# Keys loaded by tokens, key features ahead of their copies, a reordered head and a transposed last group in a polysketch-attention and ELU-MLP kernel

One core of one Trainium2 chip. The metric is the device time of one execution in microseconds (us), median of several runs. A run's span (first to last recorded activity) is about 1.9 us shorter than its time.

## The reference

```python
def phi(x):                                    # r = 8, head_dim = 32
    a = einsum('rd,bhsd->bhsr', S1, x); b = einsum('rd,bhsd->bhsr', S2, x)
    return einsum('bhsi,bhsj->bhsij', a, b).reshape(..., 64)
q_p, k_p = phi(q), phi(k)                      # q, k, v: (4, 4, 1088, 32), fp32
kv = einsum('bhsf,bhsd->bhfd', k_p, v);  z = sum(k_p, axis=2)
x  = (q_p @ kv) / (q_p . z + 1e-6)             # then heads side by side: (4352, 128)
h  = x @ w_in                                  # w_in (128, 2048), as float64
g  = where(h > 0, h, exp(min(h, 0)) - 1)
out = g @ w_out                                # w_out (2048, 128), as float64
```

The kernel calls the four batches "banks" (b = 0 to 3). S1, S2 and the weights arrive as float64 and are turned into float32 on the chip by integer operations, "rounding" below.

## The kernel before

It works through 9 groups of 512 tokens (the last has 256). One step is one group with one 256-wide piece of the weights: two matmuls into `h`, the ELU on ScalarE and VectorE, and, two steps later, two matmuls into `o`. (The traces show each of these fp32 matmuls as two records.) Names in the traces: `kT` and `qT` are the transposed keys and queries, `abp` the key features in PSUM and `ab` their copy, `kp` their products, `kv` the product with v, `gg` the output of the ELU, `oT` the running sum of `o`. All other work (keys, queries, rounding) is put between steps. Cut to what matters (`# ...` marks cuts):

```python
# keys of bank 0: one queue for each half of the partitions
for i, eng in enumerate((nc.sync, nc.scalar)):
    eng.dma_start(hd["k", 0][64 * i:64 * i + 64]..., k[0, 2 * i:2 * i + 2]...)
load_hd(nc.sync, "q", q, 0, 0, 8)
# ...
load_v(nc.sync, 0)

# the rounding of one piece: A, B (ScalarE), C, D, E; E on GpSimd if pool
order = [(0, 1, 0), (1, 1, 1), (0, 0, 1)] + [(cp, 1, 1) for cp in range(2, NP)]  # piece, w_in, w_out
def RC(i, pool=False):
    round_w(round_c, i); round_w(round_d, i); round_w(round_e, i, pool)

def KF(b, gi):                       # key features of token tiles KG[gi]
    if gi < 2:
        abps[b] = psum.tile([P, 512], F32, name="abp", tag="aux")
    abp = abps[b] if gi < 2 else abps[b][:, 256:]      # gi 2 shares the bank of gi 1
    # ... matmuls into abp, then
    nc.scalar.copy(ab..., abp...)

# last group: o (features on partitions) -> copy -> two transposes -> copy -> two DMAs
nc.vector.tensor_copy(oT[g][:, :n], o)
# ... fin2: transposes into otp, copy to osb
for u in range(2):
    for b, t, i, m in runs(g, u, 0, n):
        nc.sync.dma_start(rows[b, :, t:t + m, :], o[64 * u:64 * u + 64, i:i + m, :])

# what lies between the steps
for n, i in ((2, 3), (3, 4), (5, 5), (6, 6), (8, 7), (9, 8)):
    if i > 3: at(n - 1, RA, i); late(n - 1, RB, i)
    at(n, RC, i, i > 4)
for b in range(1, B):
    at(n - 1, transp, kT, "k", b, 0, NT)
    for i in range(3):
        at(n, KF, b, i); at(n + (i > 0), KO, b, i); at(n + 2, KA, b, i)
    # ...
```

Only one PSUM bank serves `o`; an o that opens a segment waits until the sum before it has been taken out (`oT += o` on VectorE, or a copy).

## Time and profile before

| | before |
|---|---|
| time, median of the 3 runs at hand | 299.99 us (299.66 to 300.33) |
| profiled run | 298.3 us, span 296.4 us |
| TensorE (PE) busy, share of the span | 284.5 us, 96% |
| VectorE (DVE) / ScalarE (ACT) busy | 168.0 / 188.1 us |
| mean granted TensorE clock of the profiled run | 0.991 |

In the timeline views below, a row is start, length, engine, line, operation, tiles, count, and in brackets the idle time before it and what ended it; in the chain views it is start, length, engine, tile, line.

### The profile page before, as it was taken

What the parts mean: (1) busy time and instruction counts of PE and PEld (TensorE: products, weight loads), DVE (VectorE), ACT (ScalarE), POOL (GpSimd) and SP (SyncE); (2) the same over time, 40 slices, a digit from 0 to 9 for tenths busy, and PEclk for the clock granted to TensorE, in tenths of its full rate; (3) what the DMA queues carried; (4) which work ended last, traced back from release to release, by engine and by line L of the source; (5) the groups of instructions that cost most, each with busy time, mean ns of one, the idle gap of its engine ahead of it and who ended that gap; (6) DMA issues with size and microseconds to landing.
All of it is one profiled execution on the core that took longest, in us unless ns stands there. A gap on an engine that the chain in (4) does not pass through costs nothing.

```text
span 296.4 us, 4034 instructions
## 1 busy us (share of the span) xinstructions
PE 284.5 (96%) x1448; PEld 146.0 (49%) x1448; DVE 168.0 (57%) x296; ACT 188.1 (63%) x355; POOL 19.0 (6%) x46
## 2 busy tenths in 40 slices
PE   6879989999999999999999999999999999999993
PEld 4854444544544653445544644444444444444682
DVE  4789999964657275425457274435543554355441
ACT  2249888566467467666646557766666686667681
POOL 1110034620000010000000100000000000000000
PEclk9799999999999999999999999999999999999998
DMA  6942999220110100011001100011002000110010
GB/s 157 339 157 88 198 208 217 39 75 0 18 20 9 30 0 0 3 16 19 1 2 16 21 0 0 1 18 19 0 0 31 8 0 1 17 21 0 6 30 18
DMA packets 37907, 13.37 MB, mean 45 GB/s; under 512 B 32768, under 2 KB 35968, under 8 KB 37888
## 3 DMA queue, kind: packets, MB, share of 16 engines
q1 hardware_dynamic: 37792, 12.84, 19.9%
q10 hardware_dynamic: 96, 0.28, 0.4%
q8 instruction: 11, 0.18, 0.3%
q14 instruction: 8, 0.07, 0.1%
HBM read 10.88 MB, written 2.23 MB: 44 GB/s over the span
## 4 chain that ended last, share of the span: by engine, by line
PE 86%; DVE 8%; DMA 3%; issue 1%; ACT 1%; ACTq 0%; DVEq 0%; SPq 0%
PE o L527 38%; PE h L497 35%; PE kv L300 3%; PE abp L273 2%; PE abwp L367 2%; PE xps L475 2%; PE qtp L460 2%; DMA hd_k<-in_k_dram 2%; DVE gg L514 1%; DMA raw<-in_moe_w_out_dram 1%; DVE W L114 1%; DVE kT L233 1%; DVE raw L119 1%; DVE raw L115 1%; DVE W L101 1%
## 5 line engine op out<-in xcount | busy, mean ns | idle before, releaser
L514 DVE SCALAR_TENSOR_TENSOR gg<-e,h 128x512 f32<-128x512 f32 (+1 forms) x144 | 93.0, 654 | 101.5 <-ACT e L508 101.4
L527 PE MATMUL o<-gg,W 128*128 128x512 f32 (+1 forms) x288 | 130.3, 576 | 0.0
L497 PE MATMUL h<-xg,W 128*128 128x512 f32 (+1 forms) x288 | 128.7, 569 | 0.9 <-ACT xg L446 0.5
L506 ACT ACTIVATE e<-h 128x512 f32<-128x512 f32 (+1 forms) x144 | 81.5, 566 | 23.7 <-PE h L497 23.2
L508 ACT ACTIVATE e<-e 128x512 f32<-128x512 f32 (+1 forms) x144 | 87.3, 606 | 4.5
L497 PEld LDWEIGHTS h<-xg,W 128*128 128x128 f32 x288 | 54.4, 190 | 63.6 <-issue 54.9
L527 PEld LDWEIGHTS o<-gg,W 128*128 128x128 f32 x288 | 52.5, 190 | 52.3 <-issue 48.8
L461 ACT COPY qpT<-qtp 128x512 f32<-128x512 f32 (+1 forms) x16 | 8.3, 562 | 17.1 <-PE qtp L460 17.1
L372 ACT COPY abw<-abwp 128x384 f32<-128x384 f32 (+1 forms) x8 | 3.7, 459 | 23.7 <-PE abwp L367 23.7
L257 DVE TENSOR_TENSOR kp<-ab 128x1024 f32<-128x1024 f32 (+1 forms) x12 | 11.0, 948 | 5.4 <-ACT ab L277 5.4
L277 ACT COPY ab<-abp 128x256 f32<-128x256 f32 (+1 forms) x12 | 3.8, 317 | 12.9 <-PE abp L273 12.6
L273 PE MATMUL abp<-Sab,kT 128*64 128x64 f32 x136 | 7.1, 247 | 3.4 <-DVE Sab L242 1.4
L300 PEld LDWEIGHTS kv<-v,kp 128*64 128x64 f32 (+1 forms) x288 | 9.0, 137 | 2.6 <-issue 2.3
L300 PE MATMUL kv<-v,kp 128*64 128x33 f32 (+3 forms) x288 | 9.7, 224 | 0.0
L390 DVE TENSOR_TENSOR qp<-an,abw 128x1024 f32<-128x1024 f32 (+1 forms) x9 | 9.3, 1046 | 0.3
L273 PEld LDWEIGHTS abp<-Sab,kT 128*64 128x64 f32 x136 | 5.9, 157 | 6.7 <-issue 2.6
L460 PEld LDWEIGHTS qtp<-ident,qp 128*128 128x128 f32 x60 | 7.0, 143 | 4.4 <-issue 2.8
L486 ACT COPY xg<-xps 128x256 f32<-128x256 f32 (+1 forms) x8 | 2.9, 359 | 9.5 <-PE xps L475 9.5
L460 PE MATMUL qtp<-ident,qp 128*128 128x128 f32 x60 | 8.1, 275 | 0.8 <-DVE qp L390 0.8
L320 POOL TENSOR_TENSOR zm<-kvz,zmask 128x32 f32<-128x32 f32 x4 | 1.5, 384 | 112.8 <-issue 64.5
L106 ACT ACTIVATE W<-W,ebias 128x512 uint32<-128x512 uint32 (+1 forms) x9 | 6.0, 672 | 2.7 <-DVE W L101 2.7
L124 POOL TENSOR_TENSOR raw<-raw,tiny 128x512 f32<-128x512 f32 x4 | 5.3, 1318 | 32.0 <-DVE raw L119 31.9
(82 smaller groups left out, 125.0 us busy)
## 6 DMA issues: line engine op xcount, KB each, us to landing
raw<-in_moe_w_in_dram SPq DMA_DIRECT2D x8, 256.0 KB, 6.0
raw<-in_moe_w_out_dram SPq DMA_DIRECT2D x8, 256.0 KB, 6.1
out_dram<-ob SPq DMA_DIRECT2D x104, 16.0 KB, 1.5
hd_k<-in_k_dram SPq DMA_DIRECT2D x3, 544.0 KB, 6.1
hd_q<-in_q_dram SPq DMA_DIRECT2D x3, 544.0 KB, 3.9
v<-in_v_dram SPq DMA_DIRECT2D x12, 72.0 KB, 5.6
v<-in_v_dram SPq DMA_DIRECT2D x12, 64.0 KB, 3.8
v<-in_v_dram SPq DMA_DIRECT2D x1, 288.0 KB, 5.9
```

The costliest lines, as they stand in the source:

```text
L106: nc.scalar.activation(d, d, RELU, scale=8.0, bias=ebias[:dst.shape[0]])
L257: nc.vector.tensor_mul(dst, _ap(a_, list(a_.ap[1:]) + [[0, R]]), _ap(b_, [b_.ap[1], [0, R], b_.ap[2]]))
L273: nc.tensor.matmul(abp[64 * u:64 * u + 64, j * 64:j * 64 + 64], kT[b][:, u * KT + i, :], Sab[:].rearrange("p h y -> p (h y)"), skip_group_ ...
L300: nc.tensor.matmul(kv[64 * hp:64 * hp + 64, g2, :n], kp[:rows, j, h].rearrange("p i j -> p (i j)"), _ap(vt[b][:rows, off:off + D], [[VN - ...
L390: nc.vector.tensor_mul(qp[g][:, h], _ap(a_, list(a_.ap[1:]) + [[0, R]]), _ap(b_, [b_.ap[1], [0, R], b_.ap[2]]))
L460: nc.tensor.transpose(p[:, o:o + P], qp[g][:, r:r + 2].rearrange("p t i j -> p (t i j)"), ident[:])
L461: nc.scalar.copy(qpT[g][:, 2 * hh:2 * hh + 2, :nh, :], p[:, :2 * nh * P].rearrange("p (h m s) -> p h m s", h=2, m=nh))
L497: nc.tensor.matmul(hs[g, cp][c][:, :n], W[:, cp, c * P:c * P + P], xg[g][:, :n])
L506: nc.scalar.activation(e, hs[g, cp][c][:, :n], RELU, scale=-1.0)
L508: nc.scalar.activation(e, e, EXP, scale=-1.0)
L514: nc.vector.scalar_tensor_tensor(gs[g, cp][:, c, :n], es[g, cp][:, c, :n], -1.0, hs[g, cp][c][:, :n], op0=ADD, op1=MAX)
L527: nc.tensor.matmul(ops[g][:, :n], W[:, cp, (2 + c) * P:(3 + c) * P], gg[:, c, :n], start=(first and c == 0), stop=(last and c == 1))
```

## The change

Its intent: get the keys onto the chip in a shape in which VectorE can start on half the tokens, shorten the chain to the first h matmul, remove the wait between key features and their copies, round the w_in half of pieces 2 and 3 before the w_out half, and write the last group with tokens on partitions, so that its transposes go.

```diff
-    for i, eng in enumerate((nc.sync, nc.scalar)):
-        eng.dma_start(hd["k", 0][64 * i:64 * i + 64]..., k[0, 2 * i:2 * i + 2]...)
+    load_hd(nc.sync, "k", k, 0, 0, KT)
+    load_hd(nc.scalar, "k", k, 0, KT, NT)
+    load_hd(nc.sync, "q", q, 0, 0, 8)
+    load_v(0, (nc.sync, nc.scalar))
...
-    order = [(0, 1, 0), (1, 1, 1), (0, 0, 1)] + [(cp, 1, 1) for cp in range(2, NP)]
+    order = [(0, 1, 0), (1, 1, 1), (0, 0, 1), (2, 1, 0), (3, 1, 0), (2, 0, 1), (3, 0, 1)]
+    order += [(cp, 1, 1) for cp in range(4, NP)]
...
+    make_SX()                         # ahead of the key features, no longer behind them
-    def KF(b, gi):
+    def KF(b, part):
+        abp = psum.tile([P, 512], F32, name="abp", tag="aux")
+        # part 0: tiles 0-3; part 1: tiles 4-7 and 8: all matmuls first,
+        # then the copies
...
-        RC(0)                         # the product of piece 0 moves behind the normalisation
+        round_w(round_c, 0); round_w(round_d, 0)
...
+        round_w(round_e, 0)
+        q1(1)
-            nc.scalar.copy(xg[0]...); if tt == 0: q1(1)
+            (nc.scalar.copy if tt else nc.vector.tensor_copy)(xg[0]...)
...
+    def mm2_last(cp, first, last):    # gg stationary, W moving: out has tokens on partitions
+        for a in range(4):
+            c, i = (a % 2, a // 2) if last else divmod(a, 2)
+            nc.tensor.matmul(ops[g][i][:], gg[:, c, i * P:i * P + P], W[:, cp, (2 + c) * P:(3 + c) * P], ...)
+    def fin_last():                   # two half copies, two DMAs on two queues
-    keep_warm(2)
+    keep_warm(1)
-    mm1(0, 0, (0,)) ... mm1(0, 0, (1,))
+    mm1(0, 0)
-    for n, i in ((2, 3), (3, 4), (5, 5), (6, 6), (8, 7), (9, 8)):
+    for n, i in ((2, 3), (3, 4), (4, 5), (4, 6), (5, 7), (6, 8), (8, 9), (9, 10)):
-        at(n, RC, i, i > 4)
+        at(n, RC, i, i > 6)
```

More of the change, by code (lines that the diff above doesn't have):

```diff
@@ L77, in load_hd, with load_v @@
                       src[b].rearrange("h (a c t) d -> (h a) c t d", a=32, c=2)[:, :, t0:t1, :])
-    def load_v(eng, b):
-        for u in range(2):
+    def load_v(b, engs=(nc.sync, nc.sync)):
+        for u, eng in enumerate(engs):
             t0, t1 = u * KT, min(NT, u * KT + KT)
@@ L139 @@
             eng.dma_start(S16[rs, :], src)
-    hd["k", 0] = work.tile([P, 2, NT, D], F32, name="hd_k", tag="hd_k")
-    for i, eng in enumerate((nc.sync, nc.scalar)):
-        eng.dma_start(hd["k", 0][64 * i:64 * i + 64].rearrange("p c t d -> p (c t d)"),
-                      k[0, 2 * i:2 * i + 2].rearrange("h (a x) d -> (h a) (x d)", a=32))
+    load_hd(nc.sync, "k", k, 0, 0, KT)
+    load_hd(nc.scalar, "k", k, 0, KT, NT)
+    load_hd(nc.sync, "q", q, 0, 0, 8)
+    load_v(0, (nc.sync, nc.scalar))
     warm = const.tile([R, 1], F32, name="warm")
@@ L147 @@
     nc.scalar.activation(warm[:], warm[:], EXP)
-    load_hd(nc.sync, "q", q, 0, 0, 8)
     W = const.tile([P, NP, 4 * P], F32, name="W")
@@ L184, in RC @@
         round_w(round_e, i, pool)
-    load_v(nc.sync, 0)
     load_w(0, 0)
@@ L196 @@
         load_hd(nc.sync, "k", k, b, 0, NT)
-        load_v(nc.sync, b)
+        load_v(b)
         load_hd(nc.sync, "q", q, b, 0, NT)
@@ L235, with make_SX @@
     transp(kT, "k", 0, 0, KT)
+    SX = const.tile([P, FD], F32, name="SX")
+    def make_SX():
+        xps = psum.tile([P, 512], F32, name="SXps", tag="aux")
+        nc.tensor.matmul(xps[:, :FD], idr[:].rearrange("p x j -> p (x j)"), Sx[:R].rearrange("p h d -> p (h d)"))
+        nc.scalar.copy(SX[:], xps[:, :FD])
     Sab = const.tile([FD, H, 2 * R], F32, name="Sab")
@@ L244 @@
         nc.gpsimd.tensor_copy(SW[:, b, :, :2, :].rearrange("p h x r -> p h (x r)"), Sab[:])
-    SX = const.tile([P, FD], F32, name="SX")
-    def make_SX():
-        xps = psum.tile([P, 512], F32, name="SXps", tag="aux")
-        nc.tensor.matmul(xps[:, :FD], idr[:].rearrange("p x j -> p (x j)"), Sx[:R].rearrange("p h d -> p (h d)"))
-        nc.scalar.copy(SX[:], xps[:, :FD])
     def outer(dst, ab):
@@ L260 @@
     kvS = const.tile([P, B, H, D], F32, name="kvS")
-    abps, kv_ps, feats, zms, kvz = {}, {}, {}, {}, {}
-    def KF(b, gi):
-        if gi < 2:
-            abps[b] = psum.tile([P, 512], F32, name="abp", tag="aux")
-        abp = abps[b] if gi < 2 else abps[b][:, 256:]
-        tiles = KG[gi]
-        n = len(tiles)
-        rows = P if tiles[-1] + KT < NT else 64
-        for j, i in enumerate(tiles):
-            for u in range(rows // 64):
-                nc.tensor.matmul(abp[64 * u:64 * u + 64, j * 64:j * 64 + 64], kT[b][:, u * KT + i, :],
-                                 Sab[:].rearrange("p h y -> p (h y)"),
-                                 skip_group_check=True, tile_position=(0, 64 * u))
-        ab = work.tile([P, 4, H, 2, R], F32, name="ab", tag="ab", bufs=3)
-        nc.scalar.copy(ab[:rows, :n].rearrange("p t h x r -> p (t h x r)"), abp[:rows, :n * 64])
-        feats[b, gi] = ab, rows
+    kv_ps, feats, zms, kvz = {}, {}, {}, {}
+    def KF(b, part):
+        abp = psum.tile([P, 512], F32, name="abp", tag="aux")
+        todo = []
+        for gi, o in ((1, 0), (2, 256)) if part else ((0, 0),):
+            tiles = KG[gi]
+            rows = P if tiles[-1] + KT < NT else 64
+            for j, i in enumerate(tiles):
+                for u in range(rows // 64):
+                    nc.tensor.matmul(abp[64 * u:64 * u + 64, o + j * 64:o + j * 64 + 64], kT[b][:, u * KT + i, :],
+                                     Sab[:].rearrange("p h y -> p (h y)"),
+                                     skip_group_check=True, tile_position=(0, 64 * u))
+            todo.append((gi, o, rows, len(tiles)))
+        for gi, o, rows, n in todo:
+            ab = work.tile([P, 4, H, 2, R], F32, name="ab", tag="ab", bufs=3)
+            nc.scalar.copy(ab[:rows, :n].rearrange("p t h x r -> p (t h x r)"), abp[:rows, o:o + n * 64])
+            feats[b, gi] = ab, rows
     def KO(b, gi):
@@ L423, in q5_first @@
         KS(0)
-        RC(0)
+        round_w(round_c, 0)
+        round_w(round_d, 0)
         KZ2(0)
@@ L445, in q5_first @@
                 nc.tensor.transpose(q[:, t * P:t * P + P], xn[:, tt, 4 * t:4 * t + 4].rearrange("p m d -> p (m d)"), ident[:])
-            nc.scalar.copy(xg[0][:, 256 * tt:256 * tt + 256], q[:, :256])
-            if tt == 0:
-                q1(1)
+            (nc.scalar.copy if tt else nc.vector.tensor_copy)(xg[0][:, 256 * tt:256 * tt + 256], q[:, :256])
     def q4(g):
@@ L540, in fin1 @@
             nc.scalar.copy(oT[g][:, :n], o)
-        if last and g == NQ - 1:
-            oT[g] = work.tile([P, 512], F32, name="oT", tag="oT")
-            nc.vector.tensor_copy(oT[g][:, :n], o)
-        elif last:
+        if last:
             ob = work.tile([P, 4, 2, 2, D], F32, name="ob", tag="ob", bufs=2)
@@ L553, in fin1 @@
                             nc.sync.dma_start(rows[b, w, q_, :, t:t + m, :], ob[32 * q_:32 * q_ + 32, i:i + m, u, w, :])
-    def fin2(g):
-        n = qn[g]
-        p = psum.tile([P, 512], F32, name="otp", tag="aux")
-        for i in range(n):
-            nc.tensor.transpose(p[:, i * P:i * P + P], oT[g][:, i * P:i * P + P], ident[:])
-        o = work.tile([P, 4, P], F32, name="osb", tag="osb", bufs=1)
-        nc.scalar.copy(o[:, :n].rearrange("p t f -> p (t f)"), p[:, :n * P])
-        rows = out.rearrange("(b y t) f -> b y t f", b=B, t=NT)
-        for u in range(2):
-            for b, t, i, m in runs(g, u, 0, n):
-                nc.sync.dma_start(rows[b, :, t:t + m, :], o[64 * u:64 * u + 64, i:i + m, :])
-    keep_warm(2)
+    def mm2_last(cp, first, last):
+        g = NQ - 1
+        if first:
+            ops[g] = [psum.tile([P, P], F32, name="ol", tag=t, bufs=k) for t, k in (("o", 1), ("aux", 2))]
+        gg = gs.pop((g, cp))
+        for a in range(4):
+            c, i = (a % 2, a // 2) if last else divmod(a, 2)
+            nc.tensor.matmul(ops[g][i][:], gg[:, c, i * P:i * P + P], W[:, cp, (2 + c) * P:(3 + c) * P],
+                             start=(first and c == 0), stop=(last and c == 1))
+    def fin_last():
+        g, n = NQ - 1, qn[NQ - 1]
+        o = work.tile([P, 2, P], F32, name="ol", tag="ol", bufs=1)
+        rows = out.rearrange("(b y t) f -> b y t f", b=B, t=NT)
+        for i, copy in enumerate((nc.scalar.copy, nc.vector.tensor_copy)):
+            copy(o[:, i, :], ops[g][i][:])
+        for u, eng in enumerate((nc.sync, nc.scalar)):
+            b, t = half_tile(g, 0, u)
+            eng.dma_start(rows[b, :, t:t + n, :], o[64 * u:64 * u + 64])
+    keep_warm(1)
     transp(kT, "k", 0, KT, NT)
@@ L574 @@
     q1_first()
-    KF(0, 2)
-    make_SX()
     KO(0, 1)
@@ L585 @@
     q5_first()
-    mm1(0, 0, (0,))
+    mm1(0, 0)
     RA(1)
     RB(1)
-    elu_a(0, 0, 0, (0,))
+    elu_a(0, 0, 0)
     q2(1, 2)
     q4(1)
-    mm1(0, 0, (1,))
-    elu_a(0, 0, 0, (1,))
     RC(1)
@@ L636 @@
         for i in range(3):
-            at(n, KF, b, i)
+            if i < 2:
+                at(n, KF, b, i)
             at(n + (i > 0), KO, b, i)
@@ L650 @@
         at(n + 6, q5, g)
-    done = {}
     N = len(steps)
-    for n in range(N + 4):
+    for n in range(N + 2):
         if 2 <= n < N:
@@ L663 @@
             g2, cp2, first, last = steps[n - 2]
-            if last:
+            if last and g2 < NQ - 1:
                 mm2(g2, cp2, first, last)
                 fin1(g2, cp2 == NP - 1)
-                if cp2 == NP - 1 and g2 == NQ - 1:
-                    done[n + 2] = g2
         if 2 <= n < N:
@@ L672 @@
             f(*a)
-        if 2 <= n < N + 2 and not last:
-            mm2(g2, cp2, first, last)
-        if n in done:
-            fin2(done[n])
+        if 2 <= n < N + 2:
+            if g2 == NQ - 1:
+                mm2_last(cp2, first, last)
+            elif not last:
+                mm2(g2, cp2, first, last)
+    fin_last()
 _INS = ['q', 'k', 'v', 'S1', 'S2', 'moe_w_in', 'moe_w_out']
```

## The prediction

> **What bounds the kernel now.** I read the page first (busy shares, clock slices, chain by engine), then the chain in order of time, then a table of engine busy time by stage, then the timeline of the first 62 us and the last 34.
>
> The page:
>
> ```profile
> PE 284.5 (96%) x1448; PEld 146.0 (49%) x1448; DVE 168.0 (57%) x296; ACT 188.1 (63%) x355; POOL 19.0 (6%) x46
> PEclk9799999999999999999999999999999999999998
> PE 86%; DVE 8%; DMA 3%; issue 1%; ACT 1%; ACTq 0%; DVEq 0%; SPq 0%
> ```
>
> TensorE is the bound: 86% of the chain that ended last. A full step is 1.72 us of h and 1.72 us of o matmuls, and no part of the change removes any of those. So a gain can come only from before the matmul stream starts, from holes in it, and from after its end. The chain in order of time shows these places (start, length, what):
>
> ```profile
> 1.36 4.86 DMA hd_k<-in_k_dram
> 7.81 1.83 PE abp L273 x29
> 11.67 2.42 PE kv L300 x72
> 20.80 1.29 DVE qp L390 x2
> 41.07 1.23 DVE kT L233
> 42.44 1.17 PE abp L273 x32
> 44.38 1.91 PE o L527 x4
> ```
>
> The keys hold everything until 6.2 us. A chain that is mostly VectorE's leads to the stream of h matmuls, which runs without a break from 24.70. At 41 us the chain goes back to VectorE: TensorE has finished the blocks before and waits for the transposed keys of bank 1. Then 32 of the 34 records of key features take 1.17 us, but the next o starts 1.94 us after the first of them. The waits name the reason, and it comes once for each of banks 1 to 3:
>
> ```profile
> PE abp L273 <- ACT ab L277: 1.4, 3, 0.5
> ```
>
> By stage (stretch, its length, busy time of PE, PEld, DVE, ACT, POOL, then clock, DMA share, GB/s):
>
> ```profile
> 7.80:11.60 3.80, 3.33 (x50) 3.05 (x51) 2.81 (x3) 1.22 (x4) 0.27 (x3) 0.55 1.08 327
> 28.00:42.00 14.00, 14.00 (x33) 5.98 (x32) 13.71 (x24) 12.12 (x22) 1.11 (x1) 1.00 0.98 208
> ```
>
> The second row decides my answer: while the weights are rounded, VectorE is busy for 13.71 of 14.00 us beside a full TensorE. There are two bounds there, and VectorE sets when kT of bank 1 is ready. The end of the chain:
>
> ```profile
> 288.61 2.60 PE o L527 x12
> 291.24 0.44 DVE oT L543
> 291.72 0.45 PE otp L559 x2
> 292.19 0.37 ACT osb L561
> ```
>
> After the last o come a copy, two transposes, a second copy and two output DMAs, both issued by SyncE from 292.59 in 1.20 us, each landing 2.0 us after its start.
>
> **What the Trainium skill says.** (1) "PSUM — Partial Sum Buffer", section on bank collisions: two engines must not access one bank and quadrant at once, and a scheduler orders them, reads against writes too. The trace agrees: the last group of key features shares its bank with the group before and waits 0.5 us for ScalarE's copy, three times. (2) "TensorE: Matmul & The Clock Gate", Part 1: the clock is halved after an idle window of about 3.4 us, and the window runs freely. The trace agrees: clock 0.50 from about 7.95 to 11.3 us after a hole at 5.7 to 7.2. (3) The same page, section "LDWEIGHTS (loading the stationary operand)": a load takes time with its columns, about 107 ns for 128. The sixteen loads of the 66-column matmuls quoted below start over 1.86 us, a pitch of 0.117 us each, so it agrees roughly. (4) "DMA: Bandwidth & Descriptors", section "Issuing engines are not separate DMA queues": a second queue saves issue time only, as all share 16 engines. The trace has DMA share 1.0 or more between 4 and 14 us, so I expect nothing of v on two queues but the 0.6 us of one issue on SyncE.
>
> **The change part by part.** *Keys by tokens, v on two queues.* SyncE's half of k landed at about 5.0 us, ScalarE's at 6.2. Now the first half by tokens can be transposed at 5.0 to 5.3, while the second half lands. VectorE's first transpose (0.78) is thus over before 6.2; only the second (0.69) follows. Key features need both halves, so they start at about 6.95 in place of 7.80: **0.85 us earlier**. Packets shrink from 4.3 KB to 1.0 or 1.15 KB; I count nothing for that.
>
> *Head reordered.* TensorE does all key features first and SX earlier; kp starts at about 8.1 instead of 9.34, kv at 9.4 instead of 11.6, though still partly on the half clock: half the records at 0.063 us, the rest at 0.034, so kv ends at 12.7 instead of 14.06. kvz follows at 12.7 instead of 14.11 (gain 1.4). From there VectorE's list: W rounding without its last product 1.15, SW 0.15, transposed q 0.8, then the normalisation, whose second half waits for TensorE (x0ps over at about 15.9) and ends at 16.8; then the product (0.4), the copy of xg (0.4) and the first rounding step (0.35). pw starts at 17.9 instead of 19.46: **1.55 us earlier**, and the list from pw to the end of piece 1 is unchanged, so mm1(0,1) starts at about 23.1 instead of 24.70.
>
> *Weights 2 and 3 in halves.* The pitch of a half and a whole piece is in the timeline (start, length):
>
> ```profile
> 15.33 1.86 PEld L432 LDWEIGHTS x0ps<-kvz,qpT 128*128 128x128 f32 x16
> 24.89 0.28 DVE L101 TENSOR_SCALAR W<-raw 128x256 uint32<-128x256 uint32 x1
> 25.09 1.28 DVE L514 SCALAR_TENSOR_TENSOR gg<-e,h 128x512 f32<-128x512 f32 x2
> 26.29 0.42 DVE L114 SCALAR_TENSOR_TENSOR W<-raw,W 128x256 uint32<-128x256 uint32 x1
> 27.89 0.42 DVE L101 TENSOR_SCALAR W<-raw 128x512 uint32<-128x512 uint32 x1
> 29.42 0.69 DVE L114 SCALAR_TENSOR_TENSOR W<-raw,W 128x512 uint32<-128x512 uint32 x1
> 31.94 0.42 DVE L101 TENSOR_SCALAR W<-raw 128x512 uint32<-128x512 uint32 x1
> ```
>
> A half costs 25.09 - 24.89 = 0.20 plus 27.89 - 26.29 = 1.60, together 1.80. A whole costs 31.94 - 29.42 = 2.52 plus 0.34 for its first step, 2.86. Two halves for a whole is +0.74, twice **+1.48 us** of VectorE, all ahead of kT of bank 1. From 27.89 to kT at 40.98 VectorE has no hole (13.09 us of pitches: gg 1.2 four times, pieces and first steps). So kT starts at 40.98 - 1.55 + 1.48 = 40.9: **the head's gain is spent by then**. TensorE, 1.6 us early, has done its ten blocks (17.3 us) at 40.4 and waits 1.8 us instead of 0.45. Of the head about **0.1 to 0.2 us** remains.
>
> *Key features of a bank ahead of its copies.* 34 records at 1.17/32 = 0.0366 us are 1.24; the hole was 1.94, and 1.88 for banks 2 and 3 (88.35 to 90.23, 154.18 to 156.06). **0.65 to 0.7 us for each of three banks, 2.0 to 2.1 in all**, in a stretch where TensorE alone is the bound, so it goes to the end whole. After bank 1 VectorE is where it was, TensorE 0.85 us ahead: kv of bank 1 then starts at 50.5, with kp ready at 50.4. That just fits.
>
> *Last group with tokens on partitions.* Removed: one copy cut to half size (0.44 to 0.29), the transposes (0.45), the second copy (0.37), and the wait of the second DMA for the first's issue (0.6), now on two queues. The last DMA starts at 291.55 instead of 293.19: **1.64 us less**. Added: gg is now the stationary operand, so each step has 8 loads of 128 columns with 128 moving columns instead of 4 with 256. At the loads' pitch 0.117 this is 0.94 us against 0.86, over 8 steps **0.5 us more** (an estimate from the pitch above). Net 1.1.
>
> Sum: 0.15 + 2.05 + 1.1 = 3.3 us, so 299.99 - 3.3 = 296.7. Because the errors of the head lie more on the side of gain (a warm clock in 7.9 to 11.3 would give VectorE 0.4 more), I say **296.5 us**.
>
> **The rivals.** *A, the head's gain goes through:* VectorE isn't behind when kT of bank 1 comes, and TensorE's 1.6 to 2.0 us early start stays. For it: the TensorE row shows no other hole from 25 to 42, and halves let o and h start sooner. Against it: 13.71 busy of 14.00. The result would be 294.5 to 295. *B, the loads of the last group don't hide:* with a pitch of 0.16 or more per record the last group grows by 3 us and eats the whole tail, giving 298.5 to 299. For it: a load record lasts 190 ns. Against it: 60 transposes with 128-column loads ran at 0.109 pitch (eight in 0.87 us), and loads overlap. *C, smaller key packets or contention from v on the second queue delay the second half of k or q by 0.5 to 1 us:* the DMA engines are full from 4 us on, which speaks for it; VectorE's backlog then shifts with it, and the result is 297 to 297.7.
>
> **Range and chances.** The bank part is nearly sure (2 us). Head between -0.8 and +1.6, tail between -0.5 and +1.6 give 294.6 to 298.4. Over 2% needs 6.0 us: even rival A with a full tail (1.6 + 0.45 + 2.05 + 1.6 = 5.7) falls short, so faster gets 0.08; slower 0.02; the same 0.90.
>
> **What would show each step right or wrong.** Right: mm1(0,1) near 23.1; TensorE idle 1.5 to 2 us for kT of bank 1 at about 42; the waits of key features for ScalarE's copies gone, and 1.25 us from first key feature to the next o in banks 2 and 3; 3.2 to 3.8 us from the last o to the end of the span instead of 5.2; o steps of the last group at 0.90 to 1.0 us. Wrong: no hole at kT (rival A); o steps over 1.2 us (B); the second transpose of kT after 6.8 us (C).

## The result

| | before | after |
|---|---|---|
| median, four runs each | 299.86 us (299.66 to 300.33) | 295.77 us (295.47 to 296.63) |
| profiled run: time, span | 298.3, 296.4 us | 295.71, 293.9 us |
| span after the last o matmul | 296.4 - 291.2 = 5.2 us | 293.9 - 289.9 = 4.0 us |

The ratio is 0.9866 (95% interval 0.9842 to 0.989): the mean time of one kernel's fast runs over that of the other's fast runs of the same rounds, so not quite the ratio of the medians quoted. The text had 296.5 us and "the same within 2%". Both hold. But the two profiled runs differ by 2.5 us in span, the timed medians by 4.1, and the text's sum was 3.3. A right total may hide wrong terms, and here it does.

The page of the changed kernel, clock slices and chain by engine:

```profile
PEclk9999999999999999999999999999999999999999
PE 78%; DVE 9%; DMA 6%; SPq 4%; issue 1%; DVEq 0%
```

The slice with a mean clock of 0.7 of before is gone. TensorE's share of the chain fell from 86% to 78%: more of the first 60 us is now VectorE's and the transfers'. The timeline of the changed kernel at the places that the prediction named:

```profile
6.26 1.15 PE L271 MATMUL abp<-Sab,kT 128*64 128x64 f32 x32 [0.29 <-DVE kT L231]
...
9.91 2.46 PE L300 MATMUL kv<-v,kp 128*64 128x64 f32 x72 [1.50 <-DVE kp L256]
...
22.74 3.70 PE L498 MATMUL h<-xg,W 128*128 128x512 f32 x8 [0.44 <-DVE W L127]
...
40.86 1.30 DVE L231 STREAM_TRANSPOSE kT<-hd_k 128x1088 f32<-128x1088 f32 x1
...
42.31 1.23 PE L271 MATMUL abp<-Sab,kT 128*64 128x64 f32 x34 [2.07 <-DVE kT L231]
...
43.47 1.98 PE L528 MATMUL o<-gg,W 128*128 128x512 f32 x4
...
59.96 0.68 DVE L537 TENSOR_TENSOR oT<-oT,o 128x512 f32<-128x512 f32 x1
...
60.69 1.98 PE L528 MATMUL o<-gg,W 128*128 128x512 f32 x4 [0.54 <-DVE oT L537]
```

The same two last places in the kernel before:

```profile
44.31 1.98 PE L527 MATMUL o<-gg,W 128*128 128x512 f32 x4
...
60.08 0.69 DVE L536 TENSOR_TENSOR oT<-oT,o 128x512 f32<-128x512 f32 x1
...
60.83 1.99 PE L527 MATMUL o<-gg,W 128*128 128x512 f32 x4
```

Read the starts against each other. h starts 24.70 - 22.74 = 1.96 us sooner. At kT of bank 1 (40.86 against 40.98) almost nothing of it is left, and TensorE idles for 2.07 us. Key features without their wait bring the lead at the next o to 44.31 - 43.47 = 0.84 us. At 60 us an o has to wait for VectorE's addition to oT, and the lead is 60.83 - 60.69 = 0.14 us. **Of head and bank 1 together, 0.14 us is left.** Later it is simpler. The chain, first before, then after:

```profile
88.35 1.11 PE abp L273 x32
...
90.23 1.91 PE o L527 x4
```

```profile
88.20 1.19 PE abp L271 x34
89.40 1.91 PE o L528 x4
```

From key features to o: 1.88 us before, 1.20 after, 0.68 us won; likewise 0.69 us for bank 3. The end of the chain after, and the two output DMAs in the timeline:

```profile
287.24 2.69 PE ol L561 x24
...
289.95 0.29 DVE ol L569
```

```profile
290.31 0.56 SPq L572 DMA_DIRECT2D out_dram<-ol  x1
290.32 0.57 ACTq L572 DMA_DIRECT2D out_dram<-ol  x1
```

The account of the 2.5 us between the traces: 0.14 (head and bank 1) + 1.37 (banks 2 and 3) - 0.23 (from the first h of the last group to the last o: 17.71 us against 17.48) + 1.2 (end). Why it is 4.1 in the timed runs is the question for the experiments.

### The profile page after: what moved, and what is told of

Read it like the earlier page. It is cut to its first block, busy times and chain, and to the rows that moved or that the text cites. A ratio compares the mean times of both kernels' runs of the same rounds, so it can differ in the third digit from the quotient of the medians.

```text
span 293.9 us, 4099 instructions
## 1 busy us (share of the span) xinstructions
PE 282.4 (96%) x1476; PEld 145.5 (50%) x1476; DVE 169.4 (58%) x307; ACT 188.1 (64%) x356; POOL 18.7 (6%) x46
## 4 chain that ended last, share of the span: by engine, by line
PE 78%; DVE 9%; DMA 6%; SPq 4%; issue 1%; DVEq 0%
PE o L528 34%; PE h L498 33%; PE ol L561 3%; SPq L88 2%; DMA raw<-in_moe_w_in_dram 2%; DVE gg L515 2%; PE xps L476 2%; PE qtp L461 2%; DMA raw<-in_moe_w_out_dram 2%; PE abwp L367 2%; DMA hd_k<-in_k_dram 2%; PE kv L300 2%; DVE W L114 1%; DVE W L101 1%; SPq L76 1%
## 5 line engine op out<-in xcount | busy, mean ns | idle before, releaser
L528 PE MATMUL o<-gg,W 128*128 128x512 f32 x256 | 122.3, 600 | 0.5 <-DVE oT L537 0.5
L528 PEld LDWEIGHTS o<-gg,W 128*128 128x128 f32 x256 | 46.6, 190 | 51.8 <-issue 48.7
L106 ACT ACTIVATE W<-W,ebias 128x256 uint32<-128x256 uint32 (+1 forms) x11 | 6.5, 601 | 5.2 <-DVE W L101 5.1
L561 PEld LDWEIGHTS ol<-W,gg 128*128 128x128 f32 x64 | 8.0, 192 | 0.6 <-DVE ob L545 0.3
L561 PE MATMUL ol<-W,gg 128*128 128x128 f32 x64 | 8.2, 277 | 0.0
L476 PE MATMUL xps<-qpT,kvS 64*32 64x128 f32 (+2 forms) x200 | 7.6, 298 | 0.2 <-ACT qpT L462 0.2
```

What stands on the lines that cost most here:

```text
L476: nc.tensor.matmul(xp[w][D * h:D * h + D, :nh * P].rearrange("p (m s) -> p m s", s=P)[:, m0:m0 + m, s], kvS[64 * w:64 * w + 64, b, h, :], ...
L528: nc.tensor.matmul(ops[g][:, :n], W[:, cp, (2 + c) * P:(3 + c) * P], gg[:, c, :n], start=(first and c == 0), stop=(last and c == 1))
L561: nc.tensor.matmul(ops[g][i][:], gg[:, c, i * P:i * P + P], W[:, cp, (2 + c) * P:(3 + c) * P], start=(first and c == 0), stop=(last and c ...
```

## The experiments

Theory V: VectorE's order holds TensorE twice (kT of bank 1, oT at 60 us), so what is won before 60 us comes out only as far as VectorE is relieved. Theory C: TensorE's clock. Holes in TensorE's work in the head keep or make its clock half in some executions; the changed head suffers less from it, and the timed difference includes this. Rivals: the key-feature waits were hidden anyway; the halves pay for themselves; the spread of the times comes from something else, such as transfers. "Before" of a job is always the kernel before on the same chip in the same job; three jobs, on three chips. All kernels gave correct results.

### e1: key features of banks 1 to 3 alone

```diff
 # before, with the new KF as KF2
-            at(n, KF, b, i)
+            if i < 2:
+                at(n, KF2, b, i)
```

> The kernel before with one part of the change: the key features of banks 1 to 3 ahead of their copies, bank 0 and all else as before. Theory on record (the wait removed goes to the end whole in every bank): 2.0 to 2.1 us less than before. Theory from the trace of the changed kernel (VectorE's backlog of weight rounding takes back what bank 1 gains, at the wait of the first o near 60 us for VectorE's oT addition, since o has one bank; banks 2 and 3 keep theirs): 1.4 us less, and o near 60.8 us starts where it did before. If bank copies were hidden anyway: 0.

Measured: 299.05 us median (296.70 to 299.16) against before's 298.29 (297.11 to 300.55); ratio 0.9997, interval 0.9949 to 1.0044. The timing settles nothing, and shows why: before's eleven runs fall into two groups, 297.1 to 298.3 and 300.1 to 300.6. Its profile fell on a slow run, and the chain shows where the time is:

```profile
11.89 4.24 PE kv L318 x72
```

The same 72 records took 2.42 us in the profiled run of before (in the prediction's chain): 59 ns each instead of 34. The code of this head is that of before. So the head has two speeds, with a matmul pitch 1.7 times as long in the slow one: first support for C. The slowness is there from the start: the four records of idle matmuls at 4.7 us take 2.08 us, in the profiled run of before 1.13. The clock column of this trace says 1.00 for these microseconds; in e2's trace, with kv at 3.88 us, it says 0.50. **I therefore take the pitch of the matmuls as the safer witness of the clock;** that both slow heads are one and the same thing is argued here, and tested in e9. Sorted by group after the fact, the five slow runs of e1 have a mean of 299.02 us and the five of before 300.24: 1.2 less, near the 1.4 of V and far from 2.05 and from 0. The part of the expectation on banks 2 and 3 holds (90.58 to 91.78, 1.20 us). That on o at 60.8 can't be judged, as the slow head moved everything.

### e2: the last group alone

The diff is `mm2_last` and `fin_last` of the change on the kernel before.

> The kernel before with the last group's new output alone. Theory on record: end of the span 1.6 us sooner after the last o, last group's o matmuls 0.5 us longer, net 1.1 us less. The two profiles say 1.2 to 1.3 less after the last o and 0.23 us longer matmuls, so 1.0. Rival (loads don't hide): 0 or slower.

Measured: 298.82 us (296.16 to 299.39), ratio 0.9984, interval 0.9932 to 1.0035: hidden by the two groups again. In its trace the last group takes 17.71 us from its first h to the last o, as in the changed kernel, and 3.8 us follow. The lowest run, 296.16, is 0.95 below before's lowest, 297.11, which fits the expected 1.0 but is one run against one. The four runs at 298.65 to 299.39 lie 1.2 below the slow group of before (means 299.06 and 300.24), again by a sorting after the fact. The 17.71 us leave no room for loads that don't hide.

### e3: the head alone

The changed kernel with pieces 2 and 3 whole, banks 1 to 3 in the old order, and the old last group.

> The head alone (keys by tokens, v on two queues, key features of bank 0 at once, SX early, reordered normalisation, mm1 of both halves); weights 2 and 3 whole, banks 1 to 3 and the last group as before. Theory (VectorE's order sets kT of bank 1 and the additions to oT): kT of bank 1 starts near 39.4 us instead of 41.0, 1.5 us less in the profile. Theory of the clock (the timed runs of before have a longer half-clock spell in the head than the profiled one, which the new head avoids): more than 2.5 us less in the timed runs, with the granted clock of before's runs lower than of these. If the head's gain is hidden by a later wait anyway: 0 to 0.3 us.

Measured: 296.16 us, and all six runs lie within 295.63 to 296.53; ratio 0.991 (0.9864 to 0.9956). kT of bank 1:

```profile
39.24 1.32 DVE L230 STREAM_TRANSPOSE kT<-hd_k 128x1088 f32<-128x1088 f32 x1
```

V expected 39.4. The span is 294.7 against 296.4, 1.7 us less: the head's gain goes through to the end when the halves don't take it. And none of six runs is in a slow group, where before had five of eleven: support for C as well. Its trace shows how: the head begins at the slow pitch here too (33 records of key features take 2.08 us, where 32 take 1.15 in the changed kernel's profile), but the pitch is short again before most of kv (2.86 us), and h of the second piece starts at 22.94, only 0.20 later than there. The traces of e4, e5 and e10 begin in the same way, with h at 22.73 to 22.80. e6 below shows that the new head can still lose kv to half clock.

### e4: the changed kernel with pieces 2 and 3 whole

```diff
-    order = [..., (0, 0, 1), (2, 1, 0), (3, 1, 0), (2, 0, 1), (3, 0, 1)] + [(cp, 1, 1) for cp in range(4, NP)]
+    order = [(0, 1, 0), (1, 1, 1), (0, 0, 1)] + [(cp, 1, 1) for cp in range(2, NP)]
-    for n, i in ((2, 3), (3, 4), (4, 5), (4, 6), (5, 7), (6, 8), (8, 9), (9, 10)):
+    for n, i in ((2, 3), (3, 4), (5, 5), (6, 6), (8, 7), (9, 8)):
...
-        at(n, RC, i, i > 6)
+        at(n, RC, i, i > 4)
```

> The changed kernel with weights 2 and 3 rounded whole again, as before. Theory on record: a half piece pair costs VectorE 0.74 us more than a whole, twice 1.48 us; so kT of bank 1 starts near 39.4 instead of 40.9, and the kernel ends 1.3 to 1.5 us sooner than the changed one: 5.4 us less than before. Rival (the halves are needed: with whole pieces h of weight 2 or 3 waits, and the gain is lost there): same as the changed kernel or slower, with a hole in TensorE before h of the fourth step near 30 us.

Measured: **293.94 us** (293.78 to 295.01), ratio to before 0.9845 (0.9802 to 0.9887). Span 292.1, 1.8 us less than the changed kernel. Timeline:

```profile
39.11 1.32 DVE L230 STREAM_TRANSPOSE kT<-hd_k 128x1088 f32<-128x1088 f32 x1
...
40.58 1.23 PE L270 MATMUL abp<-Sab,kT 128*64 128x64 f32 x34 [0.29 <-DVE kT L230]
```

kT comes 40.86 - 39.11 = 1.75 us sooner. 1.48 was expected of the instructions. In the trace of the changed kernel VectorE has one more hole in this stretch, 0.41 us at 33.0 to 33.4, for ScalarE's exponential. The head can be taken out of this comparison by counting from the h matmuls of the second piece (22.74, 22.80 in e4) to kT. With whole pieces it is 16.27 to 16.31 us in the traces of before, e1, e2, e3, e4 and e9; with halves 18.10 to 18.12 in those of the changed kernel, e5, e6, e7, e10 and e11. So **the halves cost 1.8 us, not 1.48**, whatever the head did. TensorE's hole before the key features is down from 2.07 us to about 0.45, h of pieces 2 and 3 never waited, and the rival falls. e4's 293.94 is 1.8 us below the changed kernel's 295.77 and 2.2 below e5's 296.15, which ran in other jobs.

### e5: the changed kernel once more

> The changed kernel once more, unaltered, to be compared with the others of this job on the same chip, since the kernel before runs in two groups of times (about 297.1 to 298.3 and 300.1) that come from its clock in the head. Theory of the clock: the changed kernel's runs stay together, 295.5 to 296.6, and its ratio to before depends on how many of before's runs fall in the slow group. Rival (the first ratio was a fair one): 0.986 again.

Measured: 296.15 us (295.13 to 298.59), ratio 0.9898 (0.9851 to 0.9945). So the first ratio looks a fortunate one, as C said (there all four runs of before were in the slow group, here six of eleven), though the two intervals overlap; but the runs do **not** stay together, which C in my form had wrong. Timeline of this profile, then the row of its stage table for one microsecond (busy times, then clock, DMA share, GB/s):

```profile
42.29 1.77 PE L271 MATMUL abp<-Sab,kT 128*64 128x64 f32 x34 [2.06 <-DVE kT L231]
43.99 3.05 PE L528 MATMUL o<-gg,W 128*128 128x512 f32 x4
```

```profile
44.00:45.00 1.00, 1.00 (x2) 0.49 (x2) 0.97 (x2) 0.91 (x3) 0.00 (x0) 0.50 0.58 142
```

The same wait for kT as in the first profile, but behind it the clock is 0.50 for 3.4 us (added up from the stage table), and o takes 3.05 us instead of 1.98. The hole that VectorE's backlog makes can be followed by a slow clock. Of the 1.6 us that this costs here, part is absorbed by the wait for oT at 60 us, which is gone in this trace: the span is 294.7 against 293.9.

### e6: the changed kernel with the old last group

> The changed kernel with the last group's old output. Expected from the two traces (1.25 us less after the last o, 0.23 us more matmul time): 1.0 us slower than the changed kernel of this job. Theory on record: 1.1. If the loads didn't hide: no slower.

Measured: 297.05 us (296.54 to 299.88), 0.9 slower by median than e5 of the same job, as expected, though one run of six lies at 299.88. That is the profiled one: the first queries landed late, kv ran at half clock, and so did o behind the hole (3.46 us in the timeline). I therefore read no end-to-end time from its trace. The stretch from the last o to the end is 5.2 us, against 3.9 in e5.

### e7: the changed kernel with the old key features in banks 1 to 3

> The changed kernel with the key features of banks 1 to 3 in their old order (last group after the copy of the group before, same bank of memory). On record: 2.05 us slower. From the trace (bank 1's 0.7 us is spent in the wait for VectorE's oT addition at 60 us, of which 0.54 us is idle): 1.4 to 1.6 us slower than the changed kernel of this job.

Measured: 298.58 us (296.84 to 300.13), 2.4 slower than e5 by median but 1.7 by lowest run; by their times and mean clocks (0.989 to 0.994) both kernels have runs with a slow clock somewhere, so the median doesn't decide. Its profiled run is free of half clock from 9 us on, as that of the changed kernel is, and can be laid beside it:

```profile
43.98 1.99 PE L545 MATMUL o<-gg,W 128*128 128x512 f32 x4
...
60.50 1.96 PE L545 MATMUL o<-gg,W 128*128 128x512 f32 x4
```

This o starts at 60.50, and at 60.69 in the changed kernel, although o behind bank 1 started at 43.98 and 43.47: the changed kernel's lead of 0.51 us became a lag of 0.19, which is the lag of its head in that run (h at 22.74 and 22.55; the oT addition at 59.96 and 59.76). So **the new order of bank 1 bought nothing by 60 us**. At the last o the changed kernel is 1.17 us ahead (289.93 and 291.10), so banks 2 and 3 gave 1.17 + 0.19, about 1.4. V's figure holds; the 2.05 on record does not.

### e8: e4, and VectorE's order mended twice

```diff
-        at(n - 1, transp, kT, "k", b, 0, NT)
+        extra.setdefault(n - 1, []).insert(0, (transp, kT, "k", b, 0, NT))
-        at(n + 3, transp, qT, "q", b, 0, NT)
+        at(n + 3 + (b == 1), transp, qT, "q", b, 0, NT)
```

> The changed kernel with whole weights 2 and 3 (as e4), and in addition kT of bank 1 ahead of the rounding of weight 4 on VectorE, and qT of bank 1 a step later, so that the oT addition at 58 us isn't behind it. If VectorE's order is what TensorE still waits for at 40.1 to 40.6 (0.45 us, kT) and at 58.4 to 59.0 (0.56 us, oT): both waits go, 0.8 to 1.0 us less than e4's 293.94, so 293.0. If other VectorE work just takes their place: 293.6 to 294.

Measured: **293.61 us** (293.14 to 293.96), ratio to before 0.9804 (0.9772 to 0.9837): the best version, and its six runs lie within 0.8 us (whether it is 2% faster is unclear, as the interval straddles that line). Yet it is only 0.3 below e4's median, which was on another chip. The wait for kT went. The other didn't:

```profile
41.07 1.71 DVE L114 SCALAR_TENSOR_TENSOR W<-raw,W 128x512 uint32<-128x512 uint32 x1
...
58.32 1.98 PE L527 MATMUL o<-gg,W 128*128 128x512 f32 x4 [0.66 <-DVE oT L536]
```

o still waits 0.66 us for oT. With kT moved, a rounding instruction of 0.68 us in the other traces runs beside GpSimd's products and takes 1.71. Other VectorE work took the place, the rival of this run.

### e9: the kernel before with two more idle matmuls

```diff
-    keep_warm(2)
+    keep_warm(3)
...
     KF(0, 2)
+    keep_warm(1)
     make_SX()
```

> The kernel before with two idle matmuls of 256 columns more, which touch no data of it: one behind the two before the key features, one in the 0.5 us hole before SX. Theory of the clock (holes in TensorE's head keep or make its clock half, for 3.4 us or more, which then doubles kv from 2.4 to about 4 us in the slow group of runs): fewer or no runs at 300, median nearer 297.5 to 298.3, and no run slower by more than 0.5 than before's slow group. Rival (the two groups have another cause, such as transfers): the two groups stay as they are.

Measured: 298.13 us, all six runs within 297.36 to 298.46, while before's eleven of this job had five at 299.7 to 300.6. Ratio 0.9956 (0.9922 to 0.9991). In its trace kv runs at the short pitch:

```profile
10.79 2.46 PE L300 MATMUL kv<-v,kp 128*64 128x64 f32 x72
```

Work that computes nothing makes the slow group disappear, with no part of the change in it. If six of eleven runs are fast anyway, as in before, six fast ones of six come by chance about once in 40 times (an estimate from these counts). With that reservation C is shown for the head; the idle matmuls move no data, which speaks against the rival of transfers.

### e10: the changed kernel with idle matmuls in the hole

```diff
+    def fill(k):
+        p = psum.tile([P, 512], F32, name="fill", tag="aux")
+        for _ in range(k):
+            nc.tensor.matmul(p[:, :256], some[:, :P], some[:, :256], skip_group_check=True)
...
+        if b == 1:
+            at(n, fill, 4)
```

> The changed kernel with four idle matmuls of 256 columns in the 2.06 us hole where TensorE waits for kT of bank 1. They take about 1.7 us and shorten no wait, so VectorE's times stay the same. Theory of the clock (the hole at 40.2 to 42.3 halves the clock in some runs, as in the profile of e5, where the first o after it took 3.05 us instead of 1.98): all runs within 295.1 to 296.0, none of the group near 297 and 298.6. Rival (the spread has another cause): the same spread as e5's, 295.1 to 298.6.

Measured: 295.68 us, six runs within **295.54 to 295.79**.

```profile
40.14 1.89 PE L633 MATMUL fill<-some 128*128 128x256 f32 x8
42.37 1.23 PE L271 MATMUL abp<-Sab,kT 128*64 128x64 f32 x34 [0.34 <-DVE kT L231]
43.53 1.98 PE L528 MATMUL o<-gg,W 128*128 128x512 f32 x4
```

Key features and o start where they did, since VectorE sets them; only the bad runs are gone. The spread of 3.5 us in e5's times shrinks to 0.25 us. e5 ran on another chip and this job has no run of the changed kernel without the filling, so this is weaker than e9; but in the two jobs that have it, four of ten of its runs are above 296.5. With the profiles of e5 and e6, in which the half clock comes right behind the hole, C is well supported for the hole too.

### e11: the halves alone, on the kernel before

> The kernel before with weights 2 and 3 in halves alone. Theory (VectorE is full there, 1.48 us are added ahead of kT of bank 1): kT starts near 42.5 us instead of 41.0, TensorE waits 1.9 us instead of 0.45, 1.5 us slower than before in the like clock state. Rival (the halves let h of weights 2 and 3 start sooner and pay for themselves): same time.

Measured: 305.14 us (303.08 to 305.46), ratio **1.017** (1.0126 to 1.0214), and every run has a mean clock of 0.988 or 0.989. There are two groups again, and each is 5.0 us above that of before in this job (means 303.15 against 298.18, 305.26 against 300.29). The profile fell on a slow head (kv 4.26 us, h 2.36 later than in before):

```profile
27.06 3.70 PE L498 MATMUL h<-xg,W 128*128 128x512 f32 x8 [0.38 <-DVE W L127]
...
45.16 1.31 DVE L234 STREAM_TRANSPOSE kT<-hd_k 128x1088 f32<-128x1088 f32 x1
```

That is 18.10 us from h to kT, 1.82 more than in before: V. The chain behind the hole of 2.05 us:

```profile
48.89 3.71 PE o L528 x4
52.60 2.60 PE h L498 x4
```

o takes 3.71 us instead of 1.91 and h 2.60 instead of 1.72: 2.7 us lost to half clock (the clock column says 0.50), and from kT to kv of bank 1 3.0 us more in all. 1.8 and 3.0 make 4.8 of the 5.0. The direction was as expected, the size more than three times the 1.5 that V alone gave. V sets the hole, C multiplies it. The rival falls.

## Why the prediction was right, and where it was not

**Right in mechanism.** The head's gain spent at kT of bank 1, TensorE idle for 1.8 us (2.07) at about 42: the central claim, that halves cost VectorE what the head wins, is confirmed by e3 (39.24 without halves), e4 (39.11) and e11. Rival A, the head's gain going through, came true only without the halves: e4 measured 293.9, a little below its 294.5 to 295. Banks 2 and 3 give 0.68 and 0.69 us (0.65 to 0.7 predicted).

**Right by luck: the time of kT, 40.9 (40.86 measured).** The head won 1.96 us, not 1.55 (h of the second piece at 22.74, not 23.1), and the halves cost 1.8, not 1.48: the sum of instruction pitches left out the hole that they open in VectorE's row. The two errors cancel.

**Wrong: "so it goes to the end whole", for bank 1.** The step that counts 0.65 to 0.7 us three times, and calls it nearly sure, fails at the first. I had checked only the next place where VectorE could hold TensorE (kv at 50.5, "that just fits") and not the one after it: o at 60 us needs the single bank that VectorE's oT addition empties. The term is 1.37 (traces; about 1.4 by e7), not 2.05.

**Mis-sized.** The last group's matmuls grew by 0.23 us, not 0.5: from 0.86 to 0.89 per o step. The pitch of 0.117 that I took from matmuls with 66 columns did not carry over: here it is 0.111. (By that pitch the sum should have been 0.6, not 0.5: 8 steps of 0.94 against 0.86.) The end gained 1.2, not 1.64: the DMAs start 1.58 us sooner behind the last o, but the one on ScalarE's queue took 2.3 us to land, against 2.0 before. (Of two stores issued together one takes 2.3 in all seven traces that have them, in e2 the one on SyncE's queue: it doesn't go with the queue.) The net, 1.0, is close to the 1.1 predicted. Key features of bank 0 began at 6.26, not 6.95, as the second half of k landed at about 5.4 (issued at 1.4, 4.0 us on its way) and not at 6.2.

**Missing: the state of the clock in the time before.** I noted the half clock of 7.9 to 11.3 us as a 0.4 us upside. (And point (2) on the Trainium skill was read too kindly: the length of that stretch fits the page's window, but the hole before it was 1.45 us, much shorter than an idle window of about 3.4.) Over all jobs 20 of 37 runs of before are at 299.66 to 300.55 and 17 at 297.11 to 298.43. All four runs behind 299.86 were in the slower group, while the profile that I did sums on (298.3) was in the other. Against the profile I was 0.8 us too hopeful (3.3 for 2.5). Against the timed runs, 0.8 too cautious (3.3 for 4.1), and this error hid the first. The range was also narrower than its own terms: with the head at -0.8, the tail at -0.5 and 2 us for the banks the time would be 299.3, not 298.4. Rivals B and C did not come true: o steps of 0.89 us, and the second transposition of kT at 5.52.

What stays open: what share of a window of time TensorE must be busy to keep its clock. The runs show only that holes of 2.05 to 2.07 us are followed by half clock in the traces of e5, e6 and e11, and are not in those of the changed kernel and e7. Added up from the clock columns, a stretch of half clock lasts 3.4 us (in the head of before and of e6, behind the hole in e5 and e6) or 6.8 (in the head of e2, behind the hole in e11), no other length before the tail. Which part of the new head makes its slow group rare was not separated either. The value of v on two queues was not isolated; in e5 and e8 kv waits 0.5 and 1.3 us for v, so once the rest is earlier v becomes a wait of its own.

## What to carry to other kernels

When two engines are full in the same stretch, follow each gain down to the last place where the second engine hands something to the first; checking the next one isn't enough. A cut that serves the order of use (halves of a weight) can cost more in fixed time per instruction than it wins: here 2 x 0.74 us, and the hole it made. Before comparing small changes, see whether the times of the kernel before come in groups; filling TensorE's holes with idle matmuls is a quick test for the clock, and in e10 the spread was 0.25 us, against 3.5 in e5 on another chip.

## What the Trainium skill lacked or had wrong

- "TensorE: Matmul & The Clock Gate", section on HAM oscillation and the table at its end: they warn of idle gaps above about 3 or 3.4 us, and these passages name no shorter single gap. A hole of about 2.06 us was followed by clock 0.50 in the traces of e5 (o 3.05 us instead of 1.98), e6 and e11. With the hole filled (e10) no run was slow.
- The same page, Part 1, says that the ramp is under 1% of a typical kernel and run-variable. The size agrees (two groups of the kernel before some 2 us apart, 0.7%), but for comparing small changes the advice is too mild: this is more than most parts of the change are worth, and e11 loses 2.7 us behind one hole.
- The same page gives the spacing of load and matmul pairs as about 81 ns for 128 columns, without naming a type, and none for fp32. Here, in fp32, one record of 128 columns takes 0.111 us (8 in 0.89) and one of 512 columns 0.43 (4 in 1.72), and each matmul is two records.
- Not a lack, but not used in time: "DMA: Bandwidth & Descriptors", rules for kernel authors, advises against two transfers to disjoint partition halves. The kernel before did just that. Between 4 and 5 us it moved 227 GB/s and the changed one, over all 128 partitions, 384, though other transfers differ too. (All traces with the old head have 214 to 228 there, all with the new one 364 to 384.)
